# K and V of an attention unit stored and loaded by one transfer each over 128 partitions

## The chip, the cores and the metric

The kernel runs on one core of one Trainium2 chip. The metric is the device time of one execution in microseconds. All data is float32. The engines are TensorE (PE), ScalarE (ACT), VectorE (DVE), GpSimd (POOL) and SyncE (SP), which here issues every transfer of the kernel to the 16 DMA engines of the core.

## The reference

A transformer layer over x of shape [1, 2048, 640]: layer norm, a qkv projection, attention of 32 heads of width 20 over a dilated window, an output projection with a residual, a second layer norm and a SwiGLU FFN of width 1728 with a residual. In short:

```python
qkv = layernorm(x) @ wqkv                    # [2048, 3*640]
idx = pos[:, None] - 2 * arange(8)           # 8 earlier positions, 2 apart; idx < 0 is masked
logits = einsum("bhsd,bhswd->bhsw", q, k[idx]) * 20 ** -0.5
o = einsum("bhsw,bhswd->bhsd", softmax(logits), v[idx])
h = x + o @ wo
y = layernorm(h)
out = h + (silu(y @ w_gate) * (y @ w_up)) @ w_down
```

Each of the 2048 positions looks at 8 positions of its own parity (even or odd).

## The kernel before, in words

**Layout.** The sequence is cut into 4 blocks (b) of 512 positions. In a block, partition p = 64 * parity + r holds four consecutive positions of one parity, row r of 64. The 640 channels are cut into 4 groups (g) of 160, that is 8 heads. A pair (b, g) is a unit: 16 units of the qkv projection and 16 of attention.

**Matmuls** keep float32 accuracy by splitting each operand into a rounded high part and a remainder and by adding three products. The weights' and activations' high parts are made on ScalarE, the remainders on VectorE, and TensorE does nearly all else.

**qkv(b, g)** makes q, k and v of a unit. ScalarE evicts the banks into a staging tile st (line 698; two halves used in turn). From there K goes to the DRAM tensor ksc, V to vsc and Q to qsc. ksc and vsc have the shape [4 groups, 2 parities, 1031 rows, 160 channels]: for each parity the 1024 positions behind a halo of 7 rows, which `zero_halo` fills with zeros (8 rows of 1120 floats in a transfer, line 455). The stores are at line 711: for K and for V two transfers, one for each parity, from 64 partitions of 2560 bytes.

**att_load(b, g)** loads a unit's Q, K and V (lines 742 and 747). A partition gets 11 rows of 160 floats, 7040 contiguous bytes that overlap with the next partition's: its own four positions and the 7 before. K and V each come in two transfers, one for each parity, to 64 partitions each. They land in the tile kv, which has three slots of 1760 floats, taken in turn by K and V of the units in their order.

**Attention** is on VectorE: for each unit two products of q and k (line 755) with a reduction each (760), the softmax (775 to 787, with the exponential on ScalarE), two products with v (795) with three halving additions each (804) and a transpose (811). The result goes to DRAM in small transfers (817).

**Afterwards** come the output projection (888 and 1262) and the FFN (976 and 991; for the last two blocks partly by a Winograd-like scheme, 1164 and 1435). FFN weights are loaded at line 938 into two raw buffers; their remainders are stored to a DRAM tensor lsc (967) and loaded again (962) for later blocks. Part of the output projection and of the FFN of the first two blocks runs while attention goes on.

**The order.** Every step is registered by `P.add` with its engine, the regions that it reads and writes and an estimate of its cost. The order in which all steps are issued, and with it the order of each engine's in-order queue, is a fixed list, `ORDER`, of entries (engine, index of the step on that engine, count). Waits follow from the regions: an engine waits at a step until the steps that it depends on are done, and all behind it on that engine wait too. SP's queue waits in the same way before it issues a transfer.

Step counts before: TensorE 841, ScalarE 657, VectorE 897, GpSimd 10, SP 553.

Of the kernel before, what the change touches and what calls it, by code (L numbers as in the profile page):

```python
# [19 lines left out]
NB, NJ, NG, NC = 4, 4, 4, 5  # L20
GC = D // NG
# [299 lines left out]
def nb(chunks, size):  # L321
    return (chunks / 16 * 0.042 + chunks * size / 435e3) * RATE
# [1315 lines left out]
```

## Time and profile before

| | before |
|---|---|
| median of 3 runs | 846.52 us (846.45 to 846.94) |
| the profiled execution | 847.86 us, its span 845.8 us |
| TensorE busy | 833.5 us, 99% of the span |
| VectorE busy | 753.7 us, 89% |
| ScalarE busy | 431.9 us, 51% |
| moved by DMA | 173.35 MB, mean 205 GB/s |
| granted TensorE clock | 1.00 |

Busy times are those of one profiled execution; its span runs from the first to the last instruction. Matmuls are pipelined, so a busy TensorE still contains small delays. The idle time of an engine is put down to what ended it. Idle time of an engine that does not set the end costs nothing by itself. For a transfer the profile gives the time from its issue on SP to its landing.

### The profile page before, as it was taken

To read this page: it belongs to the slowest core of one execution; us is meant where nothing else is said; L and a number is where in the kernel's file an instruction comes from. 1 tells how busy PE (TensorE), PEld (TensorE's weight loads), DVE (VectorE), ACT (ScalarE), POOL (GpSimd) and SP (SyncE) were. 2 spreads that over 40 slices of the span, in tenths; PEclk is the share of its full clock that TensorE was granted. 3 is DMA by queue.
4 is the path that set the end of the run, shared out by engine and by line. 5 is a ranking of instruction groups with operands and counts; after the bars stand their busy time and mean duration, and the time that the engine had idled before them with its cause. 6 is when DMAs were issued, how large, how long until landed. Compare 5 with 4: busy or idle time off the path is not lost.

```text
span 845.8 us, 11075 instructions
## 1 busy us (share of the span) xinstructions
PE 833.5 (99%) x4037; PEld 713.4 (84%) x4037; DVE 753.7 (89%) x974; ACT 431.9 (51%) x804; POOL 2.8 (0%) x13
## 2 busy tenths in 40 slices
PE   8999999999999999999999999999999999999998
PEld 6888888889978788888888888888788888887998
DVE  6499999999998999999999999999986756667996
ACT  7755466253772443468345339467933232335550
POOL 0000000000000000000000000000000000000000
PEclk9999999999999999999999999999999999999999
DMA  7896978757779897679989989876322223268002
GB/s 256 224 246 172 283 203 236 217 142 227 187 216 282 271 283 235 222 218 275 328 265 299 283 278 283 247 268 241 120 90 75 88 82 100 81 227 323 1 33 93
DMA packets 89158, 173.35 MB, mean 205 GB/s; under 512 B 34464, under 2 KB 51200, under 8 KB 88464
## 3 DMA queue, kind: packets, MB, share of 16 engines
q1 hardware_dynamic: 89104, 172.66, 66.8%
q8 instruction: 31, 0.51, 0.2%
q14 instruction: 23, 0.19, 0.1%
HBM read 125.09 MB, written 47.16 MB: 204 GB/s over the span
## 4 chain that ended last, share of the span: by engine, by line
PE 78%; DVE 9%; DMA 8%; ACT 2%; issue 1%; SPq 1%; DVEq 0%; ACTq 0%
PE bank L691 18%; PE bank L976 18%; PE bank L1164 15%; PE bank L991 13%; PE bank L1435 6%; PE bank L888 5%; PE bank L1262 2%; DMA kv<-ksc 2%; DVE pq L795 1%; DMA pq<-qsc 1%; DMA vsc<-st 1%; DVE pq L755 1%; DMA lsc<-rb 1%; DVE rb L952 1%; DMA psc<-fa 1%
## 5 line engine op out<-in xcount | busy, mean ns | idle before, releaser
L976 PE MATMUL bank<-shb,rb 128*128 128x512 f32 x885 | 212.5, 390 | 1.9 <-DVE fa L1015 1.5
L976 PEld LDWEIGHTS bank<-shb,rb 128*128 128x128 f32 x885 | 165.1, 188 | 37.5 <-DVE fa L1015 2.4
L991 PE MATMUL bank<-rb,acts 128*128 128x512 f32 x464 | 122.5, 391 | 0.5 <-DVE acts L1009 0.5
L991 PEld LDWEIGHTS bank<-rb,acts 128*128 128x128 f32 x464 | 86.5, 188 | 18.4 <-DVE acts L1009 0.9
L755 DVE TENSOR_TENSOR pq<-kv,pq 128x2560 f32<-128x2560 f32 x32 | 90.2, 2820 | 6.4 <-DMA pq<-qsc 3.0
L804 DVE TENSOR_TENSOR pq<-pq 128x1280 f32<-128x1280 f32 (+2 forms) x96 | 89.4, 931 | 1.8
L795 DVE TENSOR_TENSOR pq<-kv,pq 128x2560 f32<-128x2560 f32 x32 | 90.2, 2820 | 0.7
L760 DVE TENSOR_REDUCE pq<-pq 128x128 f32<-128x2560 f32 x32 | 90.0, 2812 | 0.4
L698 ACT ACTIVATE st<-bank,fa 128x128 f32<-128x128 f32 (+3 forms) x120 | 50.5, 476 | 64.4 <-PE bank L691 37.7
L888 PE MATMUL bank<-ra 128*128 128x320 f32 x360 | 56.0, 309 | 0.0
L888 PEld LDWEIGHTS bank<-ra 128*128 128x128 f32 x360 | 54.3, 188 | 1.7 <-ACT fa L891 0.2
L691 PE MATMUL bank<-ra,sha 128*128 128x480 f32 (+2 forms) x240 | 54.4, 382 | 0.7 <-DVE sha L639 0.5
L691 PE MATMUL bank<-ra,shb 128*128 128x512 f32 (+1 forms) x240 | 52.5, 378 | 0.9 <-ACT st L698 0.9
L691 PE MATMUL bank<-rb,sha 128*128 128x512 f32 (+1 forms) x240 | 52.9, 379 | 0.0
L691 PE MATMUL bank<-rb,shb 128*128 128x512 f32 (+1 forms) x230 | 51.5, 379 | 0.0
L691 PEld LDWEIGHTS bank<-ra,shb 128*128 128x128 f32 x240 | 44.9, 188 | 7.8 <-ACT st L698 1.2
L691 PEld LDWEIGHTS bank<-ra,sha 128*128 128x128 f32 x240 | 44.3, 188 | 8.0 <-DVE sha L639 0.9
L691 PEld LDWEIGHTS bank<-rb,sha 128*128 128x128 f32 x240 | 44.8, 188 | 6.5
L691 PEld LDWEIGHTS bank<-rb,shb 128*128 128x128 f32 x230 | 42.9, 188 | 6.2
L957 ACT CAST rb<-fa 128x1280 fp32r<-128x1280 f32 (+1 forms) x32 | 38.9, 1215 | 17.9 <-DMA fa<-in_ffn_dram 14.4
L1014 ACT ACTIVATE fa<-bank 128x512 f32<-128x512 f32 x30 | 17.9, 598 | 51.1 <-PE bank L976 41.5
L952 DVE TENSOR_TENSOR rb<-fa,rb 128x640 fp32r<-128x640 f32 (+1 forms) x52 | 41.9, 814 | 1.1 <-ACT rb L957 1.1
(213 smaller groups left out, 1309.0 us busy)
## 6 DMA issues: line engine op xcount, KB each, us to landing
fa<-in_ffn_dram SPq DMA_DIRECT2D x33, 960.0 KB, 5.3
kv<-ksc SPq DMA_DIRECT2D x32, 440.0 KB, 6.2
kv<-vsc SPq DMA_DIRECT2D x32, 440.0 KB, 7.7
rb<-lsc SPq DMA_DIRECT2D x15, 640.0 KB, 6.4
lsc<-rb SPq DMA_DIRECT2D x13, 640.0 KB, 7.6
rb<-lsc SPq DMA_DIRECT2D x19, 320.0 KB, 4.4
ksc<-st SPq DMA_DIRECT2D x32, 160.0 KB, 3.5
pq<-qsc SPq DMA_DIRECT2D x16, 320.0 KB, 7.0
```

The costliest lines, as they stand in the source:

```text
L691: T.matmul(banks[bk][:, 0:n], l, r_(wq(g, w, c) + shift, n), start=(p, c) == first_mm, stop=(p, c) == last_mm)
L698: P.add("ACT", act(m) + 0.06, lambda: A.activation(stage_t()[:, o : o + NJ * m].rearrange("p (t j c) -> p t j c", j=NJ, c=w)[:, :, j, :], ...
L755: P.add("DVE", dve(2560), lambda: V.tensor_tensor(pq(PROD, 2560).rearrange("p (j w c) -> p j w c", j=2, w=W), window(ko, 2 * jp), pq(qo + ...
L760: P.add("DVE", dve(2560), lambda: V.tensor_reduce(logits(lo)[:, :, 16 * jp : 16 * jp + 16].rearrange("p h n -> p n h"), pq(PROD, 2560).rea ...
L795: V.tensor_tensor(pq(PROD, 2560).rearrange("p (j n d) -> p j n d", j=2, d=DH), bass.AP(tensor=v.tensor, offset=v.offset, ap=[list(v.ap[0]) ...
L804: V.tensor_add(dst(v), v[:, :, 0:m, :], v[:, :, m : 2 * m, :])
L888: T.matmul(banks[bk][:, 0:320], l, r_(m, 320), start=p == 0 and c == 0, stop=p == 2 and c == NC - 1)
L952: low(640, lambda E, o=o: E.tensor_sub(ws(t, lo + o, 640)[p0:], fa[p0:, raw + o : raw + o + 640], ws(t, hi + o, 640)[p0:].bitcast(F32)), [ ...
L976: T.matmul(banks[bk], ws(wt, gu + 1280 * w + wid * c + col, 128), x(a, c), start=p == 0 and c == 0, stop=p == 2 and c == NC - 1)
L991: T.matmul(banks[k], l, m, start=first and p == 0, stop=stop and p == len(passes) - 1)
L1164: T.matmul(banks[bk], ws(wt, o + 2048 * w + 128 * k, 128), xv_[k](a), start=first and p == 0 and k == 0, stop=stop and p == 2 and k == n - ...
L1435: T.matmul(banks[bk0 + tp][:, 0:HN], v[:, 512 * a + 128 * tp : 512 * a + 128 * tp + 128], v[:, 1024 + HN * w : 1024 + HN * w + HN], start= ...
```

## The change

K of a unit is stored by one transfer from 128 partitions, and so is V; K and V of a unit are each loaded by one transfer to 128 partitions. The DRAM side of such a transfer has a dimension of 2 (the parity) in front of the 64 rows. The regions that the waits are worked out from follow: a load now depends on the one store of its group and block, and occupies the whole slot. SP has 489 steps, 64 fewer. `ORDER` is a new list for all engines: of TensorE's 841 steps 147 keep their place in the engine's queue (the others move by up to 37 places), of ScalarE's 657 it is 90 (up to 28), of VectorE's 897 it is 178 (up to 56).

```diff
 ORDER = (
-    (4, 2, 1), (4, 7, 1), (4, 4, 1), (2, 0, 1), (3, 1, 1), (3, 0, 1), (2, 1, 1), (1, 0, 1), (1, 10, 1), (2, 7, 1), (4, 3, 1), (2, 10, 1), (0, 0, 1), (4, 9, 1),
...
 )
...
         for nm, t in (("K", ksc), ("V", vsc)):
             P.add(
                 "SP", 0.07, lambda t=t: zero_halo(t), r=[rpq(PROD, 1120)],
-                w=[(f"{nm}{g}{a}", 0, 7) for g in range(NG) for a in range(2)], prio=6, nbytes=36e3,
+                w=[(f"{nm}{g}", 0, 7) for g in range(NG)], prio=6, nbytes=36e3,
             )
...
-            def put(par, dst, o):
+            def put(dst, o):
                 Q.dma_start(
-                    dst[g, par, 7 + 256 * b : 7 + 256 * b + 256, :].rearrange("(r j) c -> r (j c)", j=NJ),
-                    stage_t()[64 * par : 64 * par + 64, o : o + 640],
+                    dst[g, :, 7 + 256 * b : 7 + 256 * b + 256, :].rearrange("a (r j) c -> a r (j c)", j=NJ),
+                    stage_t()[:, o : o + 640],
                 )
             ko = so if n == 448 else so + 640
             for nmd, dst, o in (("K", ksc, ko), ("V", vsc, ko + 640)):
-                for par in range(2):
-                    P.add("SP", 0.65, lambda par=par, dst=dst, o=o: put(par, dst, o), r=[("ab", o, o + 640)],
-                          w=[(f"{nmd}{g}{par}", 1000 + 256 * b, 1256 + 256 * b)], prio=PR["kvs"], nbytes=nb(64, 2560))
+                P.add("SP", 0.65, lambda dst=dst, o=o: put(dst, o), r=[("ab", o, o + 640)],
+                      w=[(f"{nmd}{g}", 1000 + 256 * b, 1256 + 256 * b)], prio=PR["kvs"], nbytes=nb(128, 2560))
...
             for nmd, dst, o in (("K", ksc, ko), ("V", vsc, vo)):
-                for par in range(2):
-                    def ld(dst=dst, o=o, par=par):
-                        a = dst[g, par, 256 * b, :]
-                        Q.dma_start(kv_t()[64 * par : 64 * par + 64, o : o + 1760],
-                                    bass.AP(tensor=a.tensor, offset=a.offset, ap=[[640, 64], [1, 1760]]))
-                    lo_r = 0 if b == 0 else 1000 + 256 * (b - 1)
-                    P.add("SP", 0.45, ld, r=[(f"{nmd}{g}{par}", lo_r, 1000 + 256 * (b + 1))], w=[(f"fakv{par}", o, o + 1760)], prio=PR["atl"], nbytes=nb(64, 7040))
+                def ld(dst=dst, o=o):
+                    a = dst[g, 0, 256 * b, :]
+                    Q.dma_start(kv_t()[:, o : o + 1760],
+                                bass.AP(tensor=a.tensor, offset=a.offset, ap=[[SEQ * GC, 2], [640, 64], [1, 1760]]))
+                lo_r = 0 if b == 0 else 1000 + 256 * (b - 1)
+                P.add("SP", 0.45, ld, r=[(f"{nmd}{g}", lo_r, 1000 + 256 * (b + 1))], w=[("fakv0", o, o + 1760), ("fakv1", o, o + 1760)], prio=PR["atl"], nbytes=nb(128, 7040))
```

461 rows, old and new, of the table ORDER are left out of this document.

## The prediction

> **What bounds the kernel now.** I read the page first: busy shares, slices, DMA queues, chain.
>
> ```profile
> span 845.8 us, 11075 instructions
> PE 833.5 (99%) x4037; PEld 713.4 (84%) x4037; DVE 753.7 (89%) x974; ACT 431.9 (51%) x804; POOL 2.8 (0%) x13
> ...
> DMA  7896978757779897679989989876322223268002
> GB/s 256 224 246 172 283 203 236 217 142 227 187 216 282 271 283 235 222 218 275 328 265 299 283 278 283 247 268 241 120 90 75 88 82 100 81 227 323 1 33 93
> DMA packets 89158, 173.35 MB, mean 205 GB/s; under 512 B 34464, under 2 KB 51200, under 8 KB 88464
> ...
> q1 hardware_dynamic: 89104, 172.66, 66.8%
> ...
> PE 78%; DVE 9%; DMA 8%; ACT 2%; issue 1%; SPq 1%; DVEq 0%; ACTq 0%
> ```
>
> TensorE is busy for 833.5 of 845.8 us: it is the bound, and what shortens anything else can win back at most the 12.3 us in which it idles. The slices show the second resource: the DMA engines are 50 to over 90% busy in the first 28 slices (592 us) and mostly idle behind them. K and V are stored and loaded in that first part. The mean rate of a busy engine is 172.66 MB / (16 x 0.668 x 845.8 us) = 19.1 GB/s.
>
> Next the timeline of TensorE for its gaps (the bracket at the end), and the chain in order of time for two K/V transfers that stand in it:
>
> ```profile
> 1.88 4.23 PE L563 MATMUL bank<-rb 128*128 128x512 f32 x10 [1.88 <-POOL rb L1538]
> ...
> 82.84 6.34 PE L691 MATMUL bank<-ra,shb 128*128 128x448 f32 x30 [0.86 <-ACT st L698]
> 240.50 1.07 PE L548 MATMUL bank<-fa 128*128 128x128 f32 x8 [1.08 <-ACT st L698]
> 280.71 2.58 PE L976 MATMUL bank<-shb,rb 128*128 128x512 f32 x10 [1.50 <-DVE fa L1015]
> ```
>
> ```profile
> 72.84 7.90 DMA vsc<-st
> ...
> 260.58 13.84 DMA kv<-ksc
> ```
>
> The 0.86 us at 82.84 stand behind a V store (the evictions on ScalarE need its staging buffer), the 1.50 us at 280.71 behind a K load of 13.84 us. Long K/V transfers thus do reach TensorE, so far rarely.
>
> **The transfers, and on how many engines one runs.** The list of DMA issues (count, KB each, us to landing):
>
> ```profile
> kv<-ksc SPq DMA_DIRECT2D x32, 440.0 KB, 6.2
> kv<-vsc SPq DMA_DIRECT2D x32, 440.0 KB, 7.7
> ...
> ksc<-st SPq DMA_DIRECT2D x32, 160.0 KB, 3.5
> ...
> vsc<-st SPq DMA_DIRECT2D x32, 160.0 KB, 4.0
> ...
> osc<-pq SPq DMA_DIRECT2D x124, 40.0 KB, 4.9
> psc<-fa SPq DMA_DIRECT2D x19, 256.0 KB, 2.2
> ...
> qsc<-st SPq DMA_DIRECT2D x9, 320.0 KB, 5.2
> ...
> qsc<-st SPq DMA_DIRECT2D x7, 64.0 KB, 3.4
> pq<-fa SPq DMA_DIRECT2D x9, 40.0 KB, 2.1
> ...
> fa<-in_wqkv_dram SPq DMA_DIRECT2D x2, 32.0 KB, 3.2
> ksc<-pq SPq DMA_DIRECT2D x1, 35.0 KB
> vsc<-pq SPq DMA_DIRECT2D x1, 35.0 KB
> fa<-in_wqkv_dram SPq DMA_DIRECT2D x1, 16.0 KB, 4.9
> fa<-in_const_dram SPq DMA_DIRECT2D x1, 16.0 KB, 9.0
> ```
>
> The two halo stores (ksc<-pq, vsc<-pq) are the only rows without a time to landing. Count the packets under 512 B, 34464 by the page. The data rows that short are the 40 KB transfers (256 B runs, 160 packets each: 133 x 160 = 21280) and those of 128 B runs (7 of 64 KB, and 96 KB in the four small ones: 3584 + 768). That leaves 34464 - 25632 = 8832 packets of no data. The SP queue issues 553 transfers; 551 with 16 such packets and two with 8 give exactly 8832. I read it as one closing packet for each engine that a transfer used: 16 everywhere, 8 for the two halo stores, whose pattern has 8 rows.
>
> So the number of engines follows the shape, and the trace's one case whose outermost count is under 16 got that count. Old K/V patterns have an outermost count of 64. The new DRAM patterns are [2][64 rows]: the two parities lie 1031 rows of 160 floats apart, so they don't merge with the 64 rows (4 x 160 floats apart) into one dimension, and 2 stands outermost. The bounds are 2 engines (outermost count) and 16 (as 128 rows). The halo row is nearest, since it alone has a small outermost count: I take 2, and keep 16 as a rival.
>
> The Trainium skill (DMA: Bandwidth & Descriptors, Why a DMA increments its semaphore by 16 and not by 1) says that a transfer is spread over the largest number up to 16 that divides the slowest dimension of both patterns, on the lowest-numbered engines. By that rule all merged transfers share the same two engines; the trace agrees at its only test, the halo's 8. Its Rules for kernel authors also say that two transfers to partition halves serialize and that one over 128 partitions should be used: this speaks for the change, and would give the first rival's time below.
>
> **The change part by part.** Rates and stretches, from the windows (last two columns: DMA share, GB/s), and the DMA view of the first stretch:
>
> ```profile
> 0.00:24.00 24.00, 20.62 (x92) 16.64 (x93) 16.08 (x40) 17.47 (x39) 1.17 (x7) 1.00 0.78 264
> 24.00:250.00 226.00, 223.72 (x1103) 196.33 (x1102) 208.87 (x206) 130.97 (x294) 0.00 (x0) 1.00 0.78 211
> 250.00:536.00 286.00, 284.43 (x1346) 239.79 (x1346) 279.66 (x293) 145.14 (x220) 0.73 (x2) 1.00 0.87 270
> ...
> 771.00:775.00 4.00, 3.79 (x16) 2.93 (x16) 2.17 (x5) 2.08 (x4) 0.00 (x0) 1.00 1.05 403
> ```
>
> ```profile
> DMA packets 67634, 131.21 MB, mean 245 GB/s; under 512 B 29760, under 2 KB 42304, under 8 KB 66960
> ```
>
> ```profile
> L747 SPq DMA_DIRECT2D kv<-vsc x32: 445/490/1207, 45.2 to 535.6; - x32
> ```
>
> *Issues removed.* 64 of 553, some 0.49 us each on SP: 31 us of a queue that mostly waits. Nothing on TensorE: taken as 0 (bounds 0 and the 3.4 us of the three gaps above).
>
> *One load.* 880 KB on two engines is 450,560 bytes for each. An engine at its best moved 403 / 16 = 25.2 GB/s (window 771 to 775): 17.9 us, against 6.2 and 7.7 for today's halves. At the mean 19.1 GB/s it is 23.6 us. I take 25.2, since 7 KB rows leave little between packets; 32 loads: 572 us (755 at worst).
>
> *One store.* 320 KB: 163,840 bytes on each engine, 6.5 us (8.6 at worst); 32 stores: 208 us (275).
>
> *Everything else on those two engines.* Other transfers keep a sixteenth on each, and land only when that share has. Up to 536 us, where the last V load is issued, the engines work 0.78 x 24 + 0.78 x 226 + 0.87 x 286 = 444 us each, for 131.2 MB. K and V are 64 x (440 + 160) KB = 39.3 MB, 30% of the bytes; the other 70% are 311 us (at 25.2 GB/s 91.9 MB / 16 would be 228).
>
> *Sum.* The two engines have 572 + 208 + 311 = 1091 us of work before the last V load has landed, where the kernel takes 543 (535.6 + 7.7). Behind it stands what stands there now, 845.8 - 543 = 303 us: the last attention unit, then output projection and FFN on a TensorE with little DMA. 1091 + 303 = 1394 us.
>
> *Does attention overlap it?* Per unit VectorE does:
>
> ```profile
> L755 DVE TENSOR_TENSOR pq<-kv,pq 128x2560 f32<-128x2560 f32 x32 | 90.2, 2820 | 6.4 <-DMA pq<-qsc 3.0
> L804 DVE TENSOR_TENSOR pq<-pq 128x1280 f32<-128x1280 f32 (+2 forms) x96 | 89.4, 931 | 1.8
> L795 DVE TENSOR_TENSOR pq<-kv,pq 128x2560 f32<-128x2560 f32 x32 | 90.2, 2820 | 0.7
> L760 DVE TENSOR_REDUCE pq<-pq 128x128 f32<-128x2560 f32 x32 | 90.0, 2812 | 0.4
> ```
>
> 2 x (2.82 + 2.81 + 2.82) + 6 x 0.93 = 22.5 us. The two loads of a unit take 35.8, so with three slots of kv the next K loads beside the V products; the engines stay the bound. Dry spells I price at one short landing a unit (2.2 us, the psc row), 16 x 2.2 = 35: 1429. Bounds: none, or no overlap at all (16 x 22.5 = 360: 1754). The span is 2.1 us short of its execution's 847.9, which is 1.3 above the median (846.5): 1430.
>
> *The new order.* Every engine's list is rewritten, yet the last V load stands behind 436 of 841 TensorE steps (446 before): the 303 us remain. Transfers that waited behind a 7 us load now wait behind 18 to 36: FFN weights (two raw buffers) come late, VectorE stalls in order behind a missing K, ScalarE's evictions behind a store. All this falls while TensorE would otherwise be busy; it is in the 1091, as the same two engines serve it. Gaps may also lower the clock: the first ten matmuls took 4.23 us where ten at 280.71 took 2.58, some 1.7 us a restart; of those I add none, and leave them to the upper end.
>
> **Rivals.**
> 1. Sixteen engines, faster. Then a merged load is one 128-row transfer, which should land no later than today's second half (7.7 us). It pays where a K/V transfer ends a wait of TensorE: at most 0.86 + 1.08 + 1.50 = 3.4 us, 843 us. It decides from a landing of under 7 us. For: the skill's rule on halves, and old transfers of 64 rows used 16. Against: the halo's 8.
> 2. Sixteen engines, no gain: loads were hidden already (TensorE idles 12.3 us in all), 846.5 us.
> 3. Sixteen engines, slower by the joined wait: a store of 320 KB lands in 5.2 us (qsc row) against 3.5 and 4.0, and evictions wait for the whole; 1.2 us on the 16 units' V stores, of which a quarter reach TensorE (three of its gaps are of that kind among the dozen it has): 5 us, 851.
>
> **How the numbers follow.** Two engines: 0.85, at 1430, of its own between 1270 and 1700: below, the others at 228 (572 + 208 + 228 + 303 = 1311) and packets some 5% closer than in my row (780 x 0.05 = 39); above, no overlap (1754) or the mean rate (755 + 275 + 311 + 303 = 1644), neither of them whole. The three rivals: 0.06, 0.04, 0.05. A measurement of this kernel tells 0.2% (1.7 us) from no change: faster 0.06, within 0.04, slower 0.85 + 0.05 = 0.90. The range holds the first case and leaves out the rivals, 15 in 100, and some 5 in 100 of its own ends.
>
> **What would show it.** The issue list has kv<-ksc and kv<-vsc x16 at 880 KB, landing in 18 to 40 us, the stores x16 at 320 KB in 7 to 25. Packets under 512 B: 25632 + 423 x 16 + 64 x 2 + 2 x 8 = 32544 with two engines, 33440 with sixteen. TensorE's share falls to about 58%, its idle time before L976 and L691 traced to VectorE and ScalarE, theirs to kv and to the stores; mean DMA rate about 121 GB/s, while the last 300 us look as before. Wrong it is if a merged load lands in under 10 us. If they land late and the time is still under 1200, the two engines work on more than one packet at once; over 1700, the in-order queues run dry far more than priced.

## The result, and the profile after

The changed kernel takes 1408.49 us (median of 4 runs, 1407.15 to 1411.27), where the kernel before took 846.73 us beside it: a ratio of 1.664, with a 95% interval of 1.661 to 1.667. The forecast was 1430 us.

The page of the changed kernel, first its shares, slices and packets, then its chain of waits by engine and by line:

```profile
span 1406.9 us, 10990 instructions
PE 917.7 (65%) x4037; PEld 768.0 (55%) x4037; DVE 757.6 (54%) x974; ACT 431.8 (31%) x803; POOL 2.8 (0%) x13
...
PEclk9786766778777777669797888687788899999999
DMA  6221332122214123325442446355544662132811
...
DMA packets 87236, 173.33 MB, mean 123 GB/s; under 512 B 32544, under 2 KB 49280, under 8 KB 86544
...
q1 hardware_dynamic: 87184, 172.65, 37.2%
...
DMA 48%; PE 23%; SPq 17%; DVE 6%; ACT 3%; issue 2%; DVEq 0%; ACTq 0%
PE bank L1158 9%; SPq L811 7%; DMA fa<-in_ffn_dram 6%; DMA fa<-osc 6%; DMA rb<-lsc 6%; DMA kv<-ksc 5%; DMA pq<-qsc 4%; PE bank L985 4%; DMA osc<-pq 4%; PE bank L1429 3%; DMA lsc<-rb 3%; DMA kv<-vsc 3%; DMA ksc<-st 3%; PE bank L970 3%; DMA qsc<-st 3%; SPq L707 2%
```

TensorE, 99% busy before, is busy for 65%, and the chain that ended last is now half DMA. Yet the DMA engines are on average only 37% busy, and over the first 31 slices (1090 us) mostly at 10 to 50%. A bound that shows a third of its capacity busy is one of which only a part seems to be in use. The line of packets under 512 B says how many engines: 32544 is the number worked out for two. The chain also shows that everything waits, not K and V alone: weights (fa<-in_ffn_dram), attention results (fa<-osc), Q (pq<-qsc).

The issue list has the merged transfers. None of its rows, of any transfer, has a time to landing in this trace:

```profile
kv<-ksc SPq DMA_DIRECT2D x16, 880.0 KB
kv<-vsc SPq DMA_DIRECT2D x16, 880.0 KB
...
ksc<-st SPq DMA_DIRECT2D x16, 320.0 KB
vsc<-st SPq DMA_DIRECT2D x16, 320.0 KB
```

Landings are seen in the chain, in order of time (start, us, what), and who waited in the list of waits (us in total, times, longest):

```profile
89.53 43.69 DMA kv<-vsc
...
184.55 21.99 DMA ksc<-st
...
517.07 25.77 DMA kv<-ksc
...
592.14 38.68 DMA fa<-in_ffn_dram
```

```profile
DVE pq L749 <- DMA kv<-ksc: 152.1, 9, 22.4
ACT ra L871 <- DMA fa<-osc: 115.3, 8, 27.4
DVE pq L749 <- DMA pq<-qsc: 106.3, 6, 30.9
ACT rb L951 <- DMA fa<-in_ffn_dram: 104.1, 10, 28.2
...
ACT st L694 <- DMA qsc<-st: 85.8, 5, 26.6
ACT st L694 <- DMA ksc<-st: 75.0, 5, 29.9
```

Where the time went is told by two lines: the products with V, in the kernel before and in the changed one (durations in ns, then first and last start in us):

```profile
L795 DVE TENSOR_TENSOR pq<-kv,pq x32: 2780/2824/2829, 60.4 to 564.9; 128x2560 f32<-128x2560 f32 x32
```

```profile
L789 DVE TENSOR_TENSOR pq<-kv,pq x32: 2806/2824/2827, 133.3 to 1127.6; 128x2560 f32<-128x2560 f32 x32
```

From there to the end it is 845.8 - 564.9 = 280.9 us before and 1406.9 - 1127.6 = 279.3 after. The stretch in which K and V are moved has grown by 562.7 us, the whole span by 561.1: all of the loss lies there.

The windows of the changed kernel, split just behind the last packet of a K/V load, which ends at 1091.8 us (the last three numbers are clock, DMA share, GB/s), let the two engines be checked:

```profile
0.00:1093.00 1093.00, 612.28 (x2549) 507.13 (x2549) 506.36 (x536) 288.09 (x545) 1.89 (x9) 0.78 0.37 120
1093.00:1407.00 314.00, 305.41 (x1488) 260.89 (x1488) 251.24 (x438) 143.75 (x259) 0.93 (x4) 0.98 0.39 135
```

If two engines are busy all the time and the other 14 only with their sixteenth of other transfers, then 0.37 x 16 x 1093 = 2 x 1093 + 14 x o, so o = 306 us. The prediction had 311. This takes the two engines as always busy. The single packets of the trace need no such assumption: only K/V loads have packets of 7040 bytes, 4096 of them, and but for 15 us never more than two of these are in flight at once. Their times add up to 1192 us, 596 us on each of two engines.

### The profile page after: what moved, and what is told of

It is laid out like the page before. It is cut to its first block, busy times and chain, and to the rows that moved or that the text cites. A ratio compares the mean times of both kernels' runs of the same rounds, so it can differ in the third digit from the quotient of the medians.

```text
span 1406.9 us, 10990 instructions
## 1 busy us (share of the span) xinstructions
PE 917.7 (65%) x4037; PEld 768.0 (55%) x4037; DVE 757.6 (54%) x974; ACT 431.8 (31%) x803; POOL 2.8 (0%) x13
## 2 busy tenths in 40 slices
DMA packets 87236, 173.33 MB, mean 123 GB/s; under 512 B 32544, under 2 KB 49280, under 8 KB 86544
## 4 chain that ended last, share of the span: by engine, by line
DMA 48%; PE 23%; SPq 17%; DVE 6%; ACT 3%; issue 2%; DVEq 0%; ACTq 0%
PE bank L1158 9%; SPq L811 7%; DMA fa<-in_ffn_dram 6%; DMA fa<-osc 6%; DMA rb<-lsc 6%; DMA kv<-ksc 5%; DMA pq<-qsc 4%; PE bank L985 4%; DMA osc<-pq 4%; PE bank L1429 3%; DMA lsc<-rb 3%; DMA kv<-vsc 3%; DMA ksc<-st 3%; PE bank L970 3%; DMA qsc<-st 3%; SPq L707 2%
## 5 line engine op out<-in xcount | busy, mean ns | idle before, releaser
L970 PE MATMUL bank<-shb,rb 128*128 128x512 f32 x885 | 234.7, 416 | 92.5 <-ACT fa L1008 27.2
L970 PEld LDWEIGHTS bank<-shb,rb 128*128 128x128 f32 x885 | 178.5, 203 | 135.3 <-ACT fa L1008 28.1
L985 PE MATMUL bank<-rb,acts 128*128 128x512 f32 x464 | 132.8, 411 | 66.2 <-DVE acts L1001 28.5
L687 PE MATMUL bank<-rb,shb 128*128 128x512 f32 (+1 forms) x230 | 62.5, 436 | 85.3 <-ACT st L694 85.3
L694 ACT ACTIVATE st<-bank,fa 128x480 f32<-128x480 f32 (+3 forms) x120 | 50.1, 475 | 214.7 <-DMA qsc<-st 85.8
L687 PE MATMUL bank<-ra,shb 128*128 128x512 f32 (+1 forms) x240 | 65.4, 437 | 69.7 <-ACT st L694 69.7
L882 PE MATMUL bank<-ra 128*128 128x320 f32 x360 | 66.6, 343 | 54.1 <-ACT fa L885 34.4
L687 PEld LDWEIGHTS bank<-ra,shb 128*128 128x128 f32 x240 | 53.1, 225 | 81.6 <-ACT st L694 72.9
L882 PEld LDWEIGHTS bank<-ra 128*128 128x128 f32 x360 | 62.9, 216 | 58.4 <-ACT fa L885 35.1
L805 DVE STREAM_TRANSPOSE pq<-pq 128x320 f32<-128x320 f32 x32 | 16.2, 507 | 94.7 <-DMA osc<-pq 94.3
```

The source lines that it names most:

```text
L687: T.matmul(banks[bk][:, 0:n], l, r_(wq(g, w, c) + shift, n), start=(p, c) == first_mm, stop=(p, c) == last_mm)
L694: P.add("ACT", act(m) + 0.06, lambda: A.activation(stage_t()[:, o : o + NJ * m].rearrange("p (t j c) -> p t j c", j=NJ, c=w)[:, :, j, :], ...
L882: T.matmul(banks[bk][:, 0:320], l, r_(m, 320), start=p == 0 and c == 0, stop=p == 2 and c == NC - 1)
L970: T.matmul(banks[bk], ws(wt, gu + 1280 * w + wid * c + col, 128), x(a, c), start=p == 0 and c == 0, stop=p == 2 and c == NC - 1)
L985: T.matmul(banks[k], l, m, start=first and p == 0, stop=stop and p == len(passes) - 1)
```

## The experiments

Theory: the pattern's outermost count is the number of DMA engines, and the two engines' work sets the time. Rivals: the new order of all steps; the joined wait for all 128 partitions.

**1. One transfer, sixteen engines.** Interleave the parities over the partitions, so that 64 stands outermost.

```diff
-dst[g, :, 7 + 256 * b : 7 + 256 * b + 256, :].rearrange("a (r j) c -> a r (j c)", j=NJ),
+dst[g, :, 7 + 256 * b : 7 + 256 * b + 256, :].rearrange("a (r j) c -> r a (j c)", j=NJ),
-bass.AP(tensor=a.tensor, offset=a.offset, ap=[[SEQ * GC, 2], [640, 64], [1, 1760]]))
+bass.AP(tensor=a.tensor, offset=a.offset, ap=[[640, 64], [SEQ * GC, 2], [1, 1760]]))
-x = a(A_x.reshape(NB, 64, NJ, 2, D).transpose(0, 3, 1, 2, 4).reshape(NB, 128, NJ, D))
+x = a(A_x.reshape(NB, 64, NJ, 2, D).transpose(0, 1, 3, 2, 4).reshape(NB, 128, NJ, D))
```

The mask and the output's layout follow in the same way.

> The changed kernel with one thing other: the two parities are interleaved over the partitions (partition 2r + parity instead of 64 parity + r, in the input's layout, the mask and the output as well), so that the DRAM pattern of a K/V transfer is [64 rows][2 parities] and 64 stands outermost. Still one transfer of 128 partitions, same bytes, same order of all steps. Two-engines theory: the transfers run on 16 engines, land in 5 to 9 us, packets under 512 B are 33440, and the time is back at 846, between 838 and 856. New-order theory or joined-wait theory (one wait for all 128 partitions): it stays near 1408, or at least over 1000.

Measured: 839.94 us, ratio to before 0.992 (0.991 to 0.993). Its packets and issues:

```profile
DMA packets 88132, 173.33 MB, mean 206 GB/s; under 512 B 33440, under 2 KB 50176, under 8 KB 87440
...
kv<-ksc SPq DMA_DIRECT2D x16, 880.0 KB, 6.5
kv<-vsc SPq DMA_DIRECT2D x16, 880.0 KB, 6.9
ksc<-st SPq DMA_DIRECT2D x16, 320.0 KB, 3.2
vsc<-st SPq DMA_DIRECT2D x16, 320.0 KB, 3.1
```

Same bytes, same order, same joined wait, same 128 partitions: only which of two dimensions stands outermost differs, and 569 us with it. The packets under 512 B are 33440, as worked out for sixteen, and the transfers have a landing time again. New order and joined wait both fall.

**2. The order alone.** The kernel before (two transfers of 64 partitions, code of lines 705 to 715 and 743 to 750 as before) with the new list.

> The kernel before with the new order of all steps: each K/V transfer is still two of 64 partitions, issued one behind the other where the new list has the merged one. Two-engines theory: 846, between 838 and 856; what it differs from 846.5 is the order's own worth. New-order theory: 1300 to 1450.

Measured: 848.21 us, ratio 1.0018 (1.0002 to 1.0034). The order is worth next to nothing with the old transfers, at most 0.3% of a loss.

**3. Two engines in the old order.**

> The changed kernel (merged transfers, parity outermost) with the old order: a merged transfer stands where the later of its two halves stood. Two-engines theory: 1400, between 1330 and 1480, as the two engines have the same 1091 us of work before the last V load. New-order theory: near 846.

Measured: 1392.92 us, ratio 1.644 (1.641 to 1.647). 16 us less than in the new order; the rest is there whatever the order.

**4. Sixteen engines in the old order.** Edits of the first and the third.

> Interleaved parities (64 outermost, one transfer over 128 partitions) in the old order, merged transfers where the later of the two halves stood. Two-engines theory: 846, between 838 and 856; against the kernel before it gives the worth of the merge alone when all engines share a transfer: between -3.4 us (the three gaps of TensorE) and +5 us (joined wait). Joined-wait theory: clearly slower than 856.

Measured: 843.22 us, ratio 0.995 (0.994 to 0.997): the merge on sixteen engines, with the parities interleaved, is worth 3.8 us in the old order, and no loss by the joined wait shows.

**5 and 6. Loads alone, stores alone.** In the changed kernel the stores (5) or the loads (6) are cut into two of 64 partitions again:

```diff
-                P.add("SP", 0.65, lambda dst=dst, o=o: put(dst, o), r=[("ab", o, o + 640)],
+                for par in range(2):
+                    P.add("SP", 0.65, lambda par=par, dst=dst, o=o: put(par, dst, o), r=[("ab", o, o + 640)],
...
-                def ld(dst=dst, o=o):
+                for par in range(2):
+                    def ld(dst=dst, o=o, par=par):
```

> The changed kernel with its merged K/V loads (parity outermost), but stores as two transfers of 64 partitions; new order. Two-engines theory: the two engines have 572 us of loads, 311 of other transfers and 10.5 MB / 16 / 25.2 GB/s = 26 of stores: 909 + 303 = 1212 us, between 1130 and 1270. If the loads alone were the whole cause it would be 1408; if in-order stalls of SP and not the engines' work set the time, loads and stores would not add up.

> The changed kernel with its merged K/V stores (parity outermost), but loads as two transfers of 64 partitions; new order. Two-engines theory: 208 us of stores, 311 of others and 28.8 MB / 16 / 25.2 = 72 of loads: 591, some 48 more than the 543 of before: 894, between 850 and 960. If stores were the whole cause: 1408.

Measured: 1267.99 us with the loads on two engines, 971.41 with the stores. Each is a cause by itself, the loads the larger one: 421 and 124 us above the 847.4 of before. Together that is 545, where both at once cost 562. Both came out above what was worked out, the loads by 56 us and the stores by 77, the latter outside its range.

**7 to 10. A dial for the outermost count.** K and V of a unit lie in a region of their own, [count][128 / count rows], with a gap of 1120 floats behind each chunk so that the two dimensions can't merge. A partition's window is then its own four positions and the seven after them in its chunk, other neighbours than the reference's; sizes, counts, order and waits of the K/V transfers are those of the changed kernel:

```diff
-        ksc = dr.tile([NG, 2, SEQ, GC], F32, name="ksc")
+        CH = 4
+        CS = 32 * 640 + 1120
+        ksc = dr.tile([NG * NB * CH, CS], F32, name="ksc")
...
-                                bass.AP(tensor=a.tensor, offset=a.offset, ap=[[SEQ * GC, 2], [640, 64], [1, 1760]]))
+                                bass.AP(tensor=a.tensor, offset=a.offset, ap=[[CS, CH], [640, 128 // CH], [1, 1760]]))
```

> The same with [2 chunks][64 rows] (the window reads other neighbours than the reference's). Two-engines theory: as the changed kernel, 1408, between 1370 and 1440. If the regions of their own matter: outside of that.

> The merged transfers with 4 outermost instead of 2: K and V of each unit lie in DRAM regions of their own as [4 chunks][32 rows], each chunk followed by a gap, so a partition's window is its own four positions and the seven after them in its chunk (other neighbours than the reference's; sizes, counts, order and waits as in the changed kernel). Two-engines theory, with the outermost count as the number of engines: (572 + 208) x 2 / 4 + 311 = 701, + 303 = 1004 us, between 930 and 1060; packets under 512 B: 423 x 16 + 64 x 4 of no data instead of 64 x 2. If any small outermost count is as bad as 2: 1408.

> As the kernel with 4, but [8 chunks][16 rows] (the window reads other neighbours than the reference's). Two-engines theory: 780 x 2 / 8 + 311 = 506 us of work on the busiest engines, under the 543 that TensorE needs anyway: the engines are no longer the bound, 846 to 875 us.

> As the kernels with 4 and 8 outermost (K and V of a unit in a region of their own, gaps between the chunks, the window reads other neighbours than the reference's), now [16 chunks][8 rows]. Two-engines theory, with the outermost count as the number of engines: 16 engines, 836 to 848 as with 64 outermost. If the regions of their own or the gaps were what made 4 and 8 slower than worked out: over 880.

Measured: 1412.15 us with 2, 1093.52 with 4, 952.93 with 8, 847.27 with 16. The regions of their own change little: 2 is as the changed kernel, 16 as the kernel before (7 us above the first experiment, with K loads that land in 8.2 us instead of 6.5). The time falls with every doubling, so it is the count and not a peculiarity of 2. The packets and the products with V (the later start is the last one's), for 4 and for 8:

```profile
DMA packets 87492, 173.83 MB, mean 159 GB/s; under 512 B 32688, under 2 KB 49424, under 8 KB 86800
...
L791 DVE TENSOR_TENSOR pq<-kv,pq x32: 2803/2824/2828, 89.7 to 812.9; 128x2560 f32<-128x2560 f32 x32
```

```profile
DMA packets 87876, 174.40 MB, mean 184 GB/s; under 512 B 32944, under 2 KB 49680, under 8 KB 87184
...
L791 DVE TENSOR_TENSOR pq<-kv,pq x32: 2800/2824/2826, 71.6 to 668.8; 128x2560 f32<-128x2560 f32 x32
```

Each count of small packets is 25632 of data + 423 x 16 + 64 x the outermost count + 32 for the zeros of the gaps: 32688 with 4, 32944 with 8. So the number of engines is what was turned.

The times of 4 and 8 lie outside their ranges, though, the one 90 us above the 1004 worked out, the other 78 us above the end of its range. The stretch after the last product with V is again 279.2 and 279.1 us (spans 1092.1 and 947.9), so the excess lies in the K/V stretch. Its DMA shares, to just behind the last packet of a K/V load (777.0 and 632.3 us):

```profile
0.00:778.00 778.00, 605.04 (x2549) 502.60 (x2549) 506.00 (x536) 288.34 (x544) 1.89 (x9) 0.86 0.55 169
```

```profile
0.00:633.00 633.00, 556.09 (x2519) 466.55 (x2520) 501.76 (x534) 288.97 (x544) 1.90 (x9) 0.95 0.72 206
```

If the busy engines are full all the time, the first gives (0.55 x 16 x 778 - 4 x 778) / 12 = 311 us of other work, and 467 us of K and V on each of the four, 21.0 GB/s; the second 278 and 355 us, 13.8 GB/s on each of the eight. On two engines it was 1093 - 306 = 787 us, 25.0 GB/s. So the number of engines and the engines' work explain the order of the times; the rate of an engine, which the forecasts kept at 25.2, came out lower.

The packets of the loads show the same without taking the engines as always full. At most 4 and 8 of them are in flight at once, but for 17 and 22 us. With 2 outermost (the changed kernel), 4 and 8 a packet takes 291, 346 and 469 ns on average, where 25.2 GB/s would be 279. With these times in place of 279 for the loads alone, the work worked out for the busiest engines and the measured end of the last load packet are (us):

| | worked out before | with the loads' measured times | last load packet ends |
|---|---|---|---|
| loads on two engines (5) | 909 | 941 | 952 |
| stores on two engines (6) | 591 | 639 | 650 |
| 4 outermost | 701 | 769 | 777 |
| 8 outermost | 506 | 603 | 632 |

So most of what these forecasts missed is slower packets on engines that were busy nearly all the time, and not stalls of the in-order queues, though the last 8 to 29 us stay unexplained. The number of engines alone does not make a packet slow: on sixteen engines it takes 320 ns in the first experiment, but 459 with 16 outermost and 465 in the halves of the kernel before. What in a pattern makes the difference is open.

**11. Halves in the interleaved layout.** To see where the 7 us gained by the first experiment are from: the same, with each transfer cut into two over 64 partitions, 32 rows by 2 parities.

```diff
-                bass.AP(tensor=a.tensor, offset=a.offset, ap=[[640, 64], [SEQ * GC, 2], [1, 1760]]))
+                bass.AP(tensor=a.tensor, offset=a.offset, ap=[[640, 32], [SEQ * GC, 2], [1, 1760]]))
```

> The sixteen-engine kernel (interleaved parities, new order) with each K/V transfer cut again into two over 64 partitions (32 rows x 2 parities, outermost count 32, so 16 engines). If the 7 us that the sixteen-engine kernel gains over the kernel before come from 128 partitions in one transfer: 846 to 850, as with the new order and the old halves. If they come from the interleaved layout alone: 838 to 842.

Measured: 849.81 us, ratio 1.0038 (1.0021 to 1.0056). So the interleaved layout alone does not give the gain: 850 in halves, 840 whole. One transfer over 128 partitions alone does not seem to give it either, as the kernel with 16 outermost has that too and takes 847 (its regions differ, so this is no clean pair). The fast packets go with the two together: 320 ns on average for a load's packet, against 479 here and 459 there.

Of all versions that of the first experiment is the fastest and beats both kernels: the merge that was wanted, with the 64 rows outermost.

## Why the prediction was right

**The number of engines.** The step on which all hung was read from 8832 packets without data: the halo's eight rows ran on eight engines, so the outermost count decides. The new page has exactly the 32544 small packets named, the first experiment exactly the 33440 of sixteen engines. The rule of the Trainium skill (DMA: Bandwidth & Descriptors, Why a DMA increments its semaphore by 16 and not by 1) gave the same two engines. The traces agree with it at 2, 4, 8, 16 and 64 outermost.

**The sum.** K and V, 780 us, against 787 from the share, which takes the two engines as full; other transfers 311 against 306. The last packet of a K/V load ended at 1091.8 us, where the sum without dry spells had 1091. Behind it stood 315 us, where the sum had 303.

**What was a little off.** The dry spells, 35 us, were priced too high: none show up before the end of the last load, the stretch behind it is 12 us longer, and the forecast came out 21 us above the median. That the sum fits so well is partly luck. The loads took 596 us on each engine and not 572, which would make the 1091 a 1115; the other terms together came out 23 us too large. And with one part alone or with 4 or 8 outermost (experiments 5 to 8) the same working came out 56 to 107 us too low, as it kept one rate for an engine, 279 ns for a load's packet; the changed kernel comes near it with 291, 8 outermost does not with 469.

**What the profile was to show.** The mean DMA rate came as forecast (121, measured 123). Loads were to land in 18 to 40 us, stores in 7 to 25: the chain shows 25.8 and 43.7 for two loads and 22.0 for a store; one is beyond. TensorE's share was to be 58% and is 65%: its busy time grew from 833.5 to 917.7 us. That goes with the granted clock, which the prediction named and did not price: 0.78 in the first 1093 us. No run prices it, but TensorE waited in that stretch anyway.

**The rivals.** With sixteen engines the first of them is what happens, but its size was wrong: priced at 3.4 us from three gaps of TensorE, it is 7.1 in the new order. Its price counted three waits that the profile shows. In the first experiment's timeline the gaps behind the staging tile and behind the K load are gone, and those left after the first 20 us are

```profile
457.97 2.57 PE L970 MATMUL bank<-shb,rb 128*128 128x512 f32 x10 [0.70 <-ACT rb L951]
567.12 3.78 PE L1256 MATMUL bank<-ra 128*128 128x320 f32 x24 [0.52 <-ACT fa L1266]
772.86 2.33 PE L985 MATMUL bank<-rb,acts 128*128 128x512 f32 x9 [0.99 <-DVE acts L1003]
```

In all, the idle time of TensorE fell from 12.3 to 8.5 us, near what was priced; its busy time also fell by 2.2 us (833.5 to 831.3), which was not. A loss by the joined wait, the third rival, was not found in either order. The Trainium skill's rule for two transfers to partition halves (same page, Rules for kernel authors: use one over 128 partitions) is borne out by one pair of runs, at 850 against 840 us. Another shows nothing to gain: one transfer with 16 outermost takes 847 us, halves in the same order 848. And with 2 to 8 outermost the one transfer loses.

## What to carry to other kernels

Before two transfers are merged, write down the pattern of the DRAM side, outermost dimension first: a count of 2 there meant two DMA engines here, although the transfer covered 128 partitions. In this kernel the dimensions could be swapped by another order of the partitions, and then the merge gained 7 us. The page's count of small packets tells how many engines all transfers used. DMA that dominates the chain of waits while a third of its capacity is busy is a sign that few engines work.

## What the runs showed that was not expected

With two engines full, SP itself is held up. The time that SP needs to issue one of the small attention stores, in the kernel before and in the changed one (min, median, max in ns):

```profile
L817 SPq DMA_DIRECT2D osc<-pq x124: 303/434/1822, 67.8 to 562.5; - x124
```

```profile
L811 SPq DMA_DIRECT2D osc<-pq x124: 302/580/17184, 139.6 to 1124.4; - x124
```

An issue of up to 17.2 us blocks everything behind it on the only queue that issues transfers; SP holds 17% of the chain in the changed kernel, where it held 1%. The longest such issue is 8.5 us with 4 outermost, 5.1 with 8 and 1.5 with 16. That this adds to the time is not shown: by the share above, the two engines were full in the same stretch.

On sixteen engines, too, one pattern keeps the engines busier than another for the same bytes. Up to 536 us in the kernel before, and to just behind the last packet of a K/V load in the first experiment (518 us):

```profile
0.00:536.00 536.00, 528.77 (x2538) 452.76 (x2539) 504.60 (x538) 293.58 (x551) 1.89 (x9) 1.00 0.83 245
```

```profile
0.00:520.00 520.00, 516.54 (x2490) 445.47 (x2491) 494.81 (x524) 283.29 (x538) 1.89 (x9) 1.00 0.73 248
```

The same rate at 0.83 and at 0.73 of the engines' time: 18.4 and 21.2 GB/s for each busy engine. That the kernel before moves 64 partitions at a time is not the reason, or not alone: with 16 outermost a transfer covers 128, and a load's packet takes 459 ns there, nearly the 465 of before.
